# One inversion for both softmax sums and a new order of the first batch's twelve small products

## The chip, the cores and the metric

One core of a Trainium2 chip runs the whole kernel. The metric is the device time of one execution in microseconds (us); the profile of one execution gives the span from the first to the last instruction, some 2 us less. Engines are TensorE (PE in the profile), VectorE (DVE), ScalarE (ACT), GpSimd (POOL, which here issues all loads but two) and SyncE.

## The reference, cut to what matters

```python
def _attn_ref(q, k, v, tau):                 # B, N, C = 4, 6016, 256
    qn = q / (np.linalg.norm(q, axis=1, keepdims=True) + 1e-06)
    kn = k / (np.linalg.norm(k, axis=1, keepdims=True) + 1e-06)
    s = kn.transpose(0, 2, 1) @ qn / tau     # 256 x 256 per batch
    s = s - s.max(-1, keepdims=True)
    a = np.exp(s)
    a /= a.sum(-1, keepdims=True) + 1e-09
    return v @ a

def _moe_ref(x, w_gate, w_val, w_out):       # x: 24064 x 256, d_ff = 1536
    gate = 1.0 / (1.0 + np.exp(-(x @ w_gate)))
    val = x @ w_val
    return gate * val @ w_out
```

The kernel never forms `v @ a`. Per batch it multiplies the 256 x 256 matrix `a` into the weights, G = a·w_gate and H = a·w_val, and then runs the gated network on `v` itself.

Of the kernel before, what the change touches and what calls it, by code (L numbers as in the profile page):

```python
# [9 lines left out]
FP32 = mybir.dt.float32  # L10
# [7 lines left out]
def kernel(  # L18
# [20 lines left out]
    nc = tc.nc  # L39
    P = nc.NUM_PARTITIONS  # L40
# [8 lines left out]
    CB = C // P  # L49
    FC = DFF // P  # L50
    FG = 512
# [17 lines left out]
    def pool(name, bufs, **kw):  # L69
        return ctx.enter_context(tc.tile_pool(name=name, bufs=bufs, **kw))  # L70
# [4 lines left out]
    attp = pool("attp", 1)  # L75
# [6 lines left out]
    psg = pool("psg", 2, space=PSUM)  # L82
    psv = pool("psv", 2, space=PSUM)
    pso = pool("pso", 2, space=PSUM)
    pss = pool("pss", 1, space=PSUM)
    psm = pool("psm", 1, space=PSUM)
# [3 lines left out]
    def mm(out, lhsT, rhs, start, stop, **kw):  # L90
        nc.tensor.matmul(out, lhsT=lhsT, rhs=rhs, start=start, stop=stop, **kw)  # L91
# [23 lines left out]
    t0, nt = groups0[0]  # L115
# [15 lines left out]
    ones_bf = consts.tile([P, P], BF16)  # L131
# [26 lines left out]
    st = {}  # L158

    def invert(out, x, eps, num):  # L160
        nc.vector.tensor_scalar(out=out, in0=x, scalar1=eps, scalar2=None, op0=ALU.add)
        nc.vector.reciprocal(out, out)
# [175 lines left out]
        s.setdefault("e", []).append(e)  # L338
        s.setdefault("rrow", [])

    def sums(b, i, pl=psm, tag="m"):
        s = st[b]
        ps_r = pl.tile([P, 1], FP32, tag=tag, name="ps_r")
        for j in range(CB):
            mm(ps_r, s["e"][i][:, j, :], ones_bf[:, 0:1], j == 0, j == CB - 1)
        r = attp.tile([P, 1], FP32, tag=f"rrow{i}", name="rrow", bufs=2)
        invert(r, ps_r, 1e-9, 1.0)
        s["rrow"].append(r)

    def sums_both(b):  # L350
        s = st[b]
        ps_r = psm.tile([P, CB], FP32, tag="m", name="ps_r")
        for i in range(CB):
            for j in range(CB):
                mm(
                    ps_r[:, i : i + 1],
                    s["e"][i][:, j, :],
                    ones_bf[:, 0:1],
                    start=(i == 0 and j == 0),
                    stop=(j == CB - 1),  # L360
                    skip_group_check=True,
                )
        r = attp.tile([P, CB], FP32, tag="rrow", name="rrow", bufs=2)
        invert(r, ps_r, 1e-9, 1.0)
        s["rrow"] = [r[:, i : i + 1] for i in range(CB)]

    def gh_tiles(b):
        st[b]["gh"] = [
            [ghpool.tile([P, CB, FG], BF16, tag=f"{n}{fg}", name=f"gh_{n}{fg}") for fg in range(NFG)]
            for n in ("G", "H")  # L370
        ]

    gh_order = [(fg, w, i) for fg in range(NFG) for w in range(2) for i in range(CB)]

    def gh(b, n, pl=None, tag=None, act=None):
        s = st[b]
        fg, w, i = gh_order[n]
        ps = (pl or psm).tile([P, FG], FP32, tag=tag or "m", name="ps_gh")
        for j in range(CB):
            mm(  # L380
                ps,
                s["e"][i][:, j, :],
                w_sb[w][fg][:, j, :],
                start=(j == 0),
                stop=(j == CB - 1),
            )
        dst = s["gh"][w][fg][:, i, :]
        r = s["rrow"][i]
        if act if act is not None else n % 2 == 0:
            nc.scalar.activation(out=dst, in_=ps, func=ACT.Copy, scale=r)  # L390
        else:
            nc.vector.tensor_scalar(out=dst, in0=ps, scalar1=r, scalar2=None, op0=ALU.mult)  # L392


    vts = {}

    def transpose_v(b, ci, ps=None, late=None):

        t0, nt = chunks[ci]
        v_sb = vs.pop((b, ci))  # L400
        vT = vtpool.tile([P, TPC * CB, P], BF16, tag="vT", name="vT")
        flat = v_sb[:, :nt, :].rearrange("p t c -> p (t c)")
        if ps is None:
            nc.sync.dma_start_transpose(out=vT[:, : nt * CB, :], in_=flat)
        else:
            for n in range(nt * CB):
                nc.tensor.transpose(
                    out=ps[:, n, :], in_=flat[:, ds(n * P, P)], identity=ident_bf
                )
            half = nt * CB // 2  # L410
            (nc.scalar.copy if late is None else late)(vT[:, half : nt * CB, :], ps[:, half : nt * CB, :])
            nc.vector.tensor_copy(out=vT[:, :half, :], in_=ps[:, :half, :])
        vts[b, ci] = vT.rearrange("p (u cb) n -> p cb u n", cb=CB)

    hts = {}

    def glu(b, ci, f):
        t0, nt = chunks[ci]
        n = nt * P
        G, H = st[b]["gh"]  # L420
        vT = vts[b, ci]
        if f == 0:
            hts[b, ci] = hpool.tile([P, FC, CH], BF16, tag="hT", name="hT")
        ps_gate = psg.tile([P, CH], FP32, tag="g", name="ps_gate")
        ps_val = psv.tile([P, CH], FP32, tag="v", name="ps_val")
        for ps, w in ((ps_gate, G), (ps_val, H)):
            for ib in range(CB):
                mm(
                    ps[:, :n],
                    w[f // (FG // P)][:, ib, ds(f % (FG // P) * P, P)],  # L430
                    vT[:, ib, :nt, :],
                    start=(ib == 0),
                    stop=(ib == CB - 1),
                )
        g_sb = gpool.tile([P, CH], BF16, tag="g", name="g_sb")
        nc.scalar.activation(out=g_sb[:, :n], in_=ps_gate[:, :n], func=ACT.Sigmoid)  # L436
        nc.vector.tensor_tensor(  # L437
            out=hts[b, ci][:, f, :n], in0=ps_val[:, :n], in1=g_sb[:, :n], op=ALU.mult
        )
# [3 lines left out]
    def out_mms(b, ci, n0, n1):  # L443

        t0, nt = chunks[ci]
        hT = hts[b, ci]
        for n in range(n0, min(n1, nt * FC)):
            s, f = divmod(n, FC)
            if n == 0:
                ffn[b, ci] = opool.tile([P, TPC, C], FP32, tag="osb", name="out_sb")  # L450
            if f == 0:
                ffn["ps"] = pso.tile([P, C], FP32, tag="o", name="ps_o")
            mm(ffn["ps"], hT[:, f, ds(s * P, P)], w_out_sb[:, f, :], f == 0, f == FC - 1)
            if f == FC - 1:
                pending.append((ffn[b, ci], s, ffn["ps"], b, ci))
# [3 lines left out]
    def flush():  # L459
        while pending:  # L460
            out_sb, s, ps, b, ci = pending.pop(0)
            t0, nt = chunks[ci]
            nc.vector.tensor_copy(out=out_sb[:, s, :], in_=ps)  # L463
            if s == nt - 1:
                nc.sync.dma_start(out=out_rows[b][:, t0 : t0 + nt, :], in_=out_sb[:, :nt, :])
# [29 lines left out]
    for g, (t0, nt) in enumerate(groups0):  # L495
# [6 lines left out]
        while adds:  # L502
            w, last_sq = adds.pop()
# [28 lines left out]
    weights(0, 1)  # L532
    late = []
    transpose_v(
        0, 0, psv.tile([P, TPC * CB, P], BF16, tag="v", name="ps_tp"), lambda *a: late.append(a)
    )
    nc.scalar.copy(*late.pop())
    gh_tiles(0)
    sums(0, 0)
    gh(0, 0, psg, "g", act=False)  # L540
    sums(0, 1, pss, "s")
    gh(0, 1, psg, "g", act=True)
    gh(0, 2, psv, "v", act=False)
    gh(0, 3, psv, "v", act=True)
    nc.scalar.preload_act_table(ACT.Sigmoid)  # L545
    gh(0, 4, pso, "o", act=False)


    def side_work(b):
# [47 lines left out]
        return side  # L597


    prev = None  # L600
    for b in range(B):
        side = side_work(b)
        for ci in range(NCH):
            block = b + 1 < B and ci in (9, 10)
            for f in range(FC):
                glu(b, ci, f)
                flush()
                if prev is not None and not block:
                    out_mms(*prev, f * TPC, (f + 1) * TPC)
                for fn, a in side.get((ci, f), ()):  # L610
                    fn(*a)
                if (b, ci) == (0, 0) and f < len(gh_order) - 5:
                    gh(0, 5 + f, pso, "o")
            if prev is not None and block:
                for s in range(TPC):
                    for fn, a in side.get((ci, FC + s), ()):
                        fn(*a)
                    out_mms(*prev, s * FC, (s + 1) * FC)
                    flush()
            prev = (b, ci)  # L620
# [39 lines left out]
```

## The kernel before: what the change touches

The six pieces of G and H (three groups of 512 columns each) are cut into two row blocks, so there are twelve products, numbered 0 to 11 in the code and called first to twelfth here. Each is two matmuls of 512 columns into one bank of PSUM (a bank here is one buffer of a PSUM pool in the code: `psg`, `psv` and `pso` have two, `psm` and `pss` one), then one eviction that scales by the inverse softmax sum, on ScalarE or VectorE.

```python
gh_order = [(fg, w, i) for fg in range(NFG) for w in range(2) for i in range(CB)]   # 3 x 2 x 2

def gh(b, n, pl=None, tag=None, act=None):
    ...                                          # two matmuls into ps
    if act if act is not None else n % 2 == 0:
        nc.scalar.activation(out=dst, in_=ps, func=ACT.Copy, scale=r)
    else:
        nc.vector.tensor_scalar(out=dst, in0=ps, scalar1=r, scalar2=None, op0=ALU.mult)

def glu(b, ci, f):                               # one slot: 128 of the 1536 hidden columns
    ...
    ps_gate = psg.tile([P, CH], FP32, tag="g", name="ps_gate")     # 2 banks
    ps_val = psv.tile([P, CH], FP32, tag="v", name="ps_val")       # 2 banks
    for ps, w in ((ps_gate, G), (ps_val, H)):
        ...                                      # a pair of matmuls each
    nc.scalar.activation(out=g_sb[:, :n], in_=ps_gate[:, :n], func=ACT.Sigmoid)
    nc.vector.tensor_tensor(out=hts[b, ci][:, f, :n], in0=ps_val[:, :n], in1=g_sb[:, :n], op=ALU.mult)
...
gh_tiles(0)
sums(0, 0)                                       # sum and inversion of row block 0
gh(0, 0, psg, "g", act=False)
sums(0, 1, pss, "s")                             # sum and inversion of row block 1
gh(0, 1, psg, "g", act=True)
gh(0, 2, psv, "v", act=False)
gh(0, 3, psv, "v", act=True)
nc.scalar.preload_act_table(ACT.Sigmoid)
gh(0, 4, pso, "o", act=False)
...
for f in range(FC):                              # 12 slots to a chunk of v
    glu(b, ci, f)
    ...
    if (b, ci) == (0, 0) and f < len(gh_order) - 5:
        gh(0, 5 + f, pso, "o")                   # sixth to twelfth, slots 0 to 6; pso has 2 banks
```

The first chunk of `v` has three row tiles (matmuls of 384 columns), the others four (512). The second chunk is transposed on TensorE in slot 8 and copied from PSUM half by ScalarE and half by VectorE; later chunks are transposed by DMA. In later batches the twelve products run beside other work and the change does not touch them.

## Time and profile before

| | before |
|---|---|
| time, median of 6 runs | 830.18 us (829.89 to 830.55) |
| span of the profiled run | 827.9 us |
| first exponential starts | 35.03 us |
| first of the twelve products starts | 35.66 us |
| second chunk's first gate pair starts | 50.50 us |
| from there to the end | 777.40 us |

The table splits the run at three places: everything ahead of the first exponential is loading and the scores, which the change does not touch, the stretch of 15 us to the second chunk is where the change acts, and the rest would show whether a gain is given back. The lines behind it are in the prediction.

### The profile page before, as it was taken

Reading aid. Unit: us, or ns where it says so; the run is one execution under the profiler, and the core shown is the slowest. Engines: PE = TensorE matmul, PEld = TensorE weight load, DVE = VectorE, ACT = ScalarE, POOL = GpSimd, SP = SyncE. Lnnn points to the kernel's source line nnn. Section 1 sums busy time; section 2 is a strip of 40 time slices with the busy share of each in tenths; the row PEclk is TensorE's granted clock in tenths of the full one; section 3 lists DMA queues with packets and bytes.
Section 4 is the critical chain, followed back from the end, with each engine's and each line's share of the span. In section 5 each row is a group of like instructions: output and inputs, shape, how many; then the busy total and the mean of one; then the engine's idle time right before and its main releaser. Section 6 shows DMA issues by size and latency. Waiting matters only on the chain.

```text
span 827.9 us, 13618 instructions
## 1 busy us (share of the span) xinstructions
PE 806.3 (97%) x5120; PEld 498.2 (60%) x5132; DVE 589.7 (71%) x1025; ACT 392.0 (47%) x644; POOL 79.0 (10%) x151
## 2 busy tenths in 40 slices
PE   3899999999999999999999999999999999999998
PEld 2555666655666666665656566666656656666665
DVE  5777787777667777778757777778766666666664
ACT  3754444446544444445654444444565444444442
POOL 4532100002210100000301100000000000000000
PEclk9999999999999999999999999999999999999999
DMA  9999833229836532223965632232232423222111
GB/s 213 206 204 177 133 89 64 50 51 182 142 73 136 99 61 58 52 68 74 167 121 128 121 71 51 65 77 59 53 87 51 65 64 76 59 67 62 39 48 69
DMA packets 78130, 77.24 MB, mean 93 GB/s; under 512 B 50928, under 2 KB 56048, under 8 KB 78064
## 3 DMA queue, kind: packets, MB, share of 16 engines
q0 software_dynamic: 22768, 38.81, 28.4%
q1 hardware_dynamic: 55008, 36.97, 17.4%
q8 instruction: 40, 0.66, 0.3%
q10 hardware_dynamic: 288, 0.59, 0.2%
q14 instruction: 26, 0.21, 0.1%
HBM read 78.64 MB, written 24.64 MB: 125 GB/s over the span
## 4 chain that ended last, share of the span: by engine, by line
PE 93%; DMA 3%; DVE 1%; ACT 1%; issue 0%; POOL 0%; POOLq 0%; ACTq 0%
PE ps_o L91 30%; PE ps_val L91 29%; PE ps_gate L91 29%; PE ps_s L91 4%; DMA k_sb<-in_k_dram 3%; PE ps_gh L91 2%; DVE hT L437 1%; ACT g_sb L436 0%; DVE sq L187 0%; PE ps_n L91 0%; POOL q_sb L101 0%; PE ps_end L91 0%; ACT L545 0%; POOL k_sb L101 0%; DVE gh_G L392 0%
## 5 line engine op out<-in xcount | busy, mean ns | idle before, releaser
L437 DVE TENSOR_TENSOR hT<-ps_val,g_sb 128x512 bf16<-128x512 f32 (+1 forms) x576 | 390.7, 679 | 205.9 <-ACT g_sb L436 204.1
L436 ACT ACTIVATE g_sb<-ps_gate 128x512 bf16<-128x512 f32 (+1 forms) x576 | 338.2, 588 | 385.2 <-PE ps_gate L91 372.4
L91 PE MATMUL ps_val<-vT,gh_H 128*128 128x512 bf16 (+1 forms) x1152 | 337.7, 375 | 0.7 <-DVE gh_H L392 0.2
L91 PE MATMUL ps_gate<-vT,gh_G 128*128 128x512 bf16 (+1 forms) x1152 | 337.5, 375 | 0.2
L91 PE MATMUL ps_o<-w_out_sb,hT 128*128 128x256 bf16 x2244 | 324.3, 273 | 0.0
L91 PEld LDWEIGHTS <-hT 128*128 128x128 bf16 x2268 | 221.0, 98 | 125.3
L91 PEld LDWEIGHTS <-gh_H 128*128 128x128 bf16 x1152 | 112.7, 98 | 132.8 <-issue 1.8
L91 PEld LDWEIGHTS <-gh_G 128*128 128x128 bf16 x1152 | 112.5, 98 | 37.5 <-issue 0.2
L463 DVE COPY out_sb<-ps_o 128x256 f32<-128x256 f32 x187 | 77.3, 413 | 13.4 <-PE ps_o L91 13.4
L91 PE MATMUL ps_s<-k_sb,q_sb 128*128 128x256 bf16 x376 | 69.6, 287 | 16.4 <-DMA k_sb<-in_k_dram 9.3
L111 POOL DMA_DIRECT2D v_sb<-in_v_dram x48 | 25.6, 532 | 604.2 <-DMA vT<-v_sb 475.2
L91 PEld LDWEIGHTS <-q_sb 128*128 128x128 bf16 x376 | 38.5, 103 | 24.7 <-issue 10.3
L226 DVE TENSOR_TENSOR acc<-acc,sq 128x1024 bf16<-128x1024 bf16 (+1 forms) x66 | 44.2, 669 | 0.0
L187 DVE TENSOR_TENSOR sq<-q_sb 128x1024 bf16<-128x1024 bf16 (+2 forms) x42 | 28.0, 666 | 1.2 <-DMA q_sb<-in_q_dram 1.1
L101 POOL DMA_DIRECT2D q_sb<-in_q_dram x44 | 24.4, 555 | 29.6 <-PE ps_s L91 12.0
L101 POOL DMA_DIRECT2D k_sb<-in_k_dram x44 | 24.1, 547 | 18.0 <-DMA k_sb<-in_k_dram 9.4
L187 DVE TENSOR_TENSOR sq<-k_sb 128x1024 bf16<-128x1024 bf16 (+2 forms) x34 | 22.4, 658 | 0.2 <-DMA k_sb<-in_k_dram 0.2
L185 ACT ACTIVATE sq<-k_sb 128x1024 bf16<-128x1024 bf16 (+1 forms) x11 | 10.7, 1010 | 12.0 <-DMA k_sb<-in_k_dram 12.0
L91 PE MATMUL ps_gh<-w_val,e_sb 128*128 128x512 bf16 x45 | 13.5, 379 | 0.2
L91 PE MATMUL ps_gh<-w_gate,e_sb 128*128 128x512 bf16 x41 | 12.7, 379 | 0.4 <-DMA w_gate<-in_moe_w_gate_dram 0.2
L91 PEld LDWEIGHTS <-e_sb 128*128 128x128 bf16 x112 | 10.0, 97 | 4.5 <-ACT e_sb L327 1.0
L436 ACT ACT_TABLE_LOAD x6 | 7.7, 1283 | 9.4 <-PE ps_gate L91 9.3
(69 smaller groups left out, 122.9 us busy)
## 6 DMA issues: line engine op xcount, KB each, us to landing
out_dram<-out_sb SPq DMA_DIRECT2D x43, 512.0 KB, 2.9
v_sb<-in_v_dram POOLq DMA_DIRECT2D x44, 256.0 KB, 3.9
q_sb<-in_q_dram POOLq DMA_DIRECT2D x35, 256.0 KB, 6.6
k_sb<-in_k_dram POOLq DMA_DIRECT2D x35, 256.0 KB, 7.6
q_sb<-in_q_dram POOLq DMA_DIRECT2D x4, 512.0 KB, 11.6
k_sb<-in_k_dram POOLq DMA_DIRECT2D x4, 512.0 KB, 13.5
out_dram<-out_sb SPq DMA_DIRECT2D x5, 384.0 KB, 2.5
v_sb<-in_v_dram POOLq DMA_DIRECT2D x4, 192.0 KB, 3.5
```

The lines of the kernel that those rows point to most:

```text
L91: nc.tensor.matmul(out, lhsT=lhsT, rhs=rhs, start=start, stop=stop, **kw)
L101: nc.gpsimd.dma_start(out=tl[:, :nt, :], in_=rows(src, b)[:, t0 : t0 + nt, :])
L111: nc.gpsimd.dma_start(out=v_sb[:, :nt, :], in_=rows(v, b)[:, t0 : t0 + nt, :])
L185: nc.scalar.activation(out=sq[:, :nt, :], in_=src[:, :nt, :], func=ACT.Square)
L187: engine.tensor_tensor(out=sq[:, :nt, :], in0=src[:, :nt, :], in1=src[:, :nt, :], op=ALU.mult)
L226: nc.vector.tensor_tensor(out=acc[:, :nt, :], in0=acc[:, :nt, :], in1=st[b]["sq", w][:, :nt, :], op=ALU.add)
L436: nc.scalar.activation(out=g_sb[:, :n], in_=ps_gate[:, :n], func=ACT.Sigmoid)
L437: nc.vector.tensor_tensor(out=hts[b, ci][:, f, :n], in0=ps_val[:, :n], in1=g_sb[:, :n], op=ALU.mult)
L463: nc.vector.tensor_copy(out=out_sb[:, s, :], in_=ps)
```

## The change

It does four things, of which the title does not name the last. It inverts both sums together, after the first product's matmuls; it puts the fifth product between the gate and the value pair of slot 0; it puts the eleventh and the twelfth product into slot 5 together; and it gives the copy of the second chunk's transposed `v` whole to VectorE.

```diff
-    sums(0, 0)
-    gh(0, 0, psg, "g", act=False)
-    sums(0, 1, pss, "s")
+    ps_first = gh_mms(0, 0, psg, "g")
+    sums_both(0)
+    gh_store(0, 0, ps_first, False)
     gh(0, 1, psg, "g", act=True)
     ...
     nc.scalar.preload_act_table(ACT.Sigmoid)
-    gh(0, 4, pso, "o", act=False)
     ... (transpose_v)
-            half = nt * CB // 2
-            (nc.scalar.copy if late is None else late)(vT[:, half : nt * CB, :], ps[:, half : nt * CB, :])
+            half = nt * CB // 2 if late else nt * CB
+            if late:
+                late(vT[:, half : nt * CB, :], ps[:, half : nt * CB, :])
             nc.vector.tensor_copy(out=vT[:, :half, :], in_=ps[:, :half, :])
     ... (glu, in the loop over gate and value)
+            if between is not None and w is G:
+                between()
     ... (main loop)
+    gh_first = {f: (5 + f,) for f in range(len(gh_order) - 7)}
+    gh_first[len(gh_order) - 7] = tuple(range(len(gh_order) - 2, len(gh_order)))
-                glu(b, ci, f)
+                first = (b, ci, f) == (0, 0, 0)
+                glu(b, ci, f, (lambda: gh(0, 4, pso, "o", act=False)) if first else None)
-                if (b, ci) == (0, 0) and f < len(gh_order) - 5:
-                    gh(0, 5 + f, pso, "o")
+                if (b, ci) == (0, 0):
+                    for i in gh_first.get(f, ()):
+                        gh(0, i, pso, "o")
```

(Cuts are marked; `gh` is split into its matmuls and its eviction, and `sums` goes away.)

More of the change, by code (lines that the diff above doesn't have):

```diff
@@ L339, in exps @@
         s.setdefault("rrow", [])
-    def sums(b, i, pl=psm, tag="m"):
-        s = st[b]
-        ps_r = pl.tile([P, 1], FP32, tag=tag, name="ps_r")
-        for j in range(CB):
-            mm(ps_r, s["e"][i][:, j, :], ones_bf[:, 0:1], j == 0, j == CB - 1)
-        r = attp.tile([P, 1], FP32, tag=f"rrow{i}", name="rrow", bufs=2)
-        invert(r, ps_r, 1e-9, 1.0)
-        s["rrow"].append(r)
     def sums_both(b):
@@ L373, with gh_mms @@
     gh_order = [(fg, w, i) for fg in range(NFG) for w in range(2) for i in range(CB)]
-    def gh(b, n, pl=None, tag=None, act=None):
+    def gh_mms(b, n, pl, tag):
         s = st[b]
         fg, w, i = gh_order[n]
-        ps = (pl or psm).tile([P, FG], FP32, tag=tag or "m", name="ps_gh")
+        ps = pl.tile([P, FG], FP32, tag=tag, name="ps_gh")
         for j in range(CB):
@@ L386, in gh, with gh_store @@
             )
+        return ps
+    def gh_store(b, n, ps, act):
+        s = st[b]
+        fg, w, i = gh_order[n]
         dst = s["gh"][w][fg][:, i, :]
         r = s["rrow"][i]
-        if act if act is not None else n % 2 == 0:
+        if act:
             nc.scalar.activation(out=dst, in_=ps, func=ACT.Copy, scale=r)
@@ L392, in gh @@
             nc.vector.tensor_scalar(out=dst, in0=ps, scalar1=r, scalar2=None, op0=ALU.mult)
+    def gh(b, n, pl, tag, act=None):
+        gh_store(b, n, gh_mms(b, n, pl, tag), n % 2 == 0 if act is None else act)
     vts = {}
@@ L415, with glu @@
     hts = {}
-    def glu(b, ci, f):
+    def glu(b, ci, f, between=None):
         t0, nt = chunks[ci]
```

## The prediction

> **What bounds the kernel now.** I read the page first, then TensorE's list of waits, then the chain of work in the 20 us that the diff touches, then the timeline of TensorE, VectorE and ScalarE there.
>
> The page's first line, and what TensorE waited for in the whole run (line waited for, total us, times, longest):
>
> ```profile
> PE 806.3 (97%) x5120; PEld 498.2 (60%) x5132; DVE 589.7 (71%) x1025; ACT 392.0 (47%) x644; POOL 79.0 (10%) x151
> PE ps_s L91 <- DMA k_sb<-in_k_dram: 9.3, 6, 3.0
> PE ps_s L91 <- ACT k_sb L139: 7.0, 1, 7.0
> PE ps_r L91 <- ACT e_sb L327: 0.5, 1, 0.5
> PE ps_gh L91 <- DMA w_gate<-in_moe_w_gate_dram: 0.2, 1, 0.2
> PE ps_val L91 <- DVE gh_H L392: 0.2, 1, 0.2
> ```
>
> TensorE is busy for 806.3 of 827.9 us. Of its 21.6 us of idle time, 16.3 belong to loading the first batch, before anything that this change touches. From 50 us to the end the same list is empty. So the change, which alters only 35 to 51 us, can win at most the small holes of that stretch. The chain of work there (start, us, what):
>
> ```profile
> 35.80 0.47 PE ps_gh L91 x2
> 36.30 0.75 DVE gh_G L392
> 37.05 0.08 DVE rrow L161
> 37.15 0.18 DVE rrow L162
> 37.41 0.69 ACT gh_G L390
> 38.10 0.58 ACT gh_H L390
> 38.69 1.28 ACT L545
> 39.99 0.50 ACT g_sb L436
> 40.51 0.57 DVE hT L437
> 41.12 0.48 PE ps_val L91 x2
> ...
> 47.02 0.67 DVE gh_H L392
> 47.73 0.34 PE ps_val L91
> ```
>
> The reader is to see two excursions away from TensorE. In the first, the second inversion (37.05 to 37.33) stands behind the eviction of the first product on VectorE. ScalarE's first eviction waits for it until 37.41, and then come its second eviction, the sigmoid table's load and the first sigmoid. In the second, the value product of slot 8 waits for the twelfth product, evicted only at 47.0. The rest is in the timelines:
>
> ```profile
> 37.90 0.59 PE L91 MATMUL ps_gh<-w_gate,e_sb 128*128 128x512 bf16 x2 [0.23 <-DMA w_gate<-in_moe_w_gate_dram]
> 44.77 0.74 DVE L392 TENSOR_SCALAR gh_G<-ps_gh,rrow 128x512 bf16<-128x512 f32 x1
> 49.17 0.42 DVE L412 COPY vT<-ps_tp 128x512 bf16<-128x512 bf16 x1 [0.44 <-ACT vT L411]
> 49.65 0.49 PE L91 MATMUL ps_gate<-vT,gh_G 128*128 128x384 bf16 x2
> 50.18 0.48 PE L91 MATMUL ps_val<-vT,gh_H 128*128 128x384 bf16 x2
> ```
>
> **Holes, from starts rather than idle time.** A matmul's recorded end overlaps the next one, so I take spacing. Two 512-column matmuls follow at 0.43 us (36.18 to 36.61 and the like), two 384-column ones at 0.33 (48.35, 48.68, 49.00). Against that:
> - The fifth product starts at 37.90. The four before it, begun at 36.65, leave room from 37.52: 0.38 us lost, on a weight load.
> - Slot 2's value product starts at 41.12, its gate pair at 40.53: 0.59 less 0.33 is 0.26 lost, waiting for slot 0's product on VectorE to free its bank.
> - Slot 8's second value matmul starts at 47.73, its first at 47.22: 0.51 less 0.16 is 0.35 lost.
> - Slot 11's value pair starts at 50.18, its gate pair at 49.65: 0.53 less 0.33 is 0.20 lost, because VectorE is late after the v copy.
>
> Together 1.19 us: 0.14% of the kernel, the ceiling of the change.
>
> [...] the first gate pair, whose operand was ready at 38.10, starts at 38.33 behind the fifth product that was held to 37.90. [...] The load took 1.28 us, but it began 0.01 after the eviction before it and the sigmoid began 0.02 after it; [...] so I count 1.28. [...] VectorE's half of the v copy stood 0.44 us behind ScalarE's half of the same bank.
>
> **The change, part by part.**
>
> *One inversion.* Two tiny matmuls, one add and one reciprocal on VectorE go away as separate steps (0.15 + 0.16 us of work); the remaining pair takes 128x2 operands at 0.15 and 0.17, as later batches show. It now needs both exponentials. The second ends at 36.05; its sum matmuls started at 36.12 before and should again, ending at 36.32. Before, the sum's end (35.80) to the add's start took 0.04, and from the add's start to the scaled eviction 0.46 on VectorE (35.84 to 36.30) and 0.44 on ScalarE (36.97 to 37.41). So the add starts at 36.36, VectorE's first eviction at 36.82 instead of 36.30, ScalarE's first at 36.83 instead of 37.41. ScalarE's second is then held by its own product, whose matmuls end at 37.67 as before: it starts at 37.72 and ends at 38.40 instead of 38.68. Of 0.58 us won on the first, 0.28 reach the table load. First sigmoid: 39.71. First hT: 40.22 to 40.79. Slot 2's value product: 40.83 instead of 41.12, a gain of 0.29 that TensorE really sees.
>
> *Fifth product moved.* The gate pair now needs both G parts, ready at 37.57, and starts about 37.62 instead of 38.33. The fifth product follows at 37.95, just after its weights at 37.90. The value pair waits for H (38.40) and starts at 38.45 to 38.50 instead of 38.66. TensorE's early gain of about 0.2 lies in front of the 40.83 above, so it is inside the 0.29 and not added: it is what keeps the fifth product out of the way, not time by itself.
>
> *Last two products in one slot.* The twelfth leaves slot 6 for slot 5, about 0.9 us earlier, so slot 8 finds its H: plus 0.35. But these products have two banks. The tenth, in slot 4, is evicted by VectorE at 44.77 to 45.51, shifted by 0.29 to 44.48 to 45.22. The eleventh would start at 44.44 and the twelfth at 44.87, in the tenth's bank: it must wait to about 45.27, minus 0.40. This new wait is my main doubt.
>
> *The v copy of the second chunk*, which the short title does not name: ScalarE's half (0.58 us) goes, and VectorE copies all 1024 columns. The rows give 0.35 us for 384 columns and 0.42 for 512, so 0.57 ns a column and 0.71 us for 1024. VectorE does 0.29 more work but loses the wait of 0.44, and ScalarE is 0.58 freer for the next sigmoid. I expect slot 11's hole to close: plus 0.20.
>
> Sum: 0.29 + 0.35 + 0.20 - 0.40 = 0.44 us; without the bank wait 0.84. I take a gain of 0.55 us.
>
> **Rivals.**
> - *The bank wait takes back everything* (0.6 us or more, if the twelfth lands in the eleventh's bank or the tenth's eviction comes later than shifted). For it: only 0.43 lies between the two products against an eviction of 0.74. Against it: TensorE waiting there lets the sigmoids catch up, and slot 8's wait still goes. Time: 830.2 to 830.4.
> - *VectorE becomes the bound of the first chunk.* Per slot it has 0.56 for hT plus every other 0.74, under 1 us of the slots' 1.09 (43.00 to 44.08); the longer v copy is one step of 0.71. In slots 8 to 11, spaced 0.65, there is little room: hT of slot 9 might come late again. Then slot 11 keeps its 0.20 hole: gain 0.25, 830.05.
> - *A transfer hides the gain.* The DMA queues are full until 70 us. But q of batch 1 was issued at 37.18 with a median of 12.3 us to landing, so it is there by about 49.5, first used at 54.40. The third chunk's v transpose was issued at 48.23 and took 15.7, so it lands at 63.9 and is first needed at 66.10: 2.2 us of slack against a shift below 1.2. This would have to fail by more than 1 us; I give it little. Time then 830.3.
> - *Everything closes*: 1.19 us, 829.1. Against: the table load still stands in series after 38.40.
>
> **Range and chances.** 830.3 less 0.55 is 829.75. Mechanisms spread from 829.1 to 830.4. Three runs of the same kernel spread over 829.89 to 830.55, so 0.3 to 0.5 us of run-to-run noise goes on both sides: 828.9 to 830.7. A 2% change is 16.6 us, fourteen times all the holes that the change can reach: within 2% is 0.99, and the rest covers a mistake about the later batches, whose program I read as unchanged.
>
> **What would show it.** One inversion of 128x2 starting at about 36.36; ScalarE's first eviction at 36.83 and the table load at about 38.41; the first gate pair at 37.6 and the fifth product between it and its value pair; slot 2's value pair at about 40.83; a hole of about 0.4 before the twelfth product; none in slots 8 and 11; one v copy of 128x1024 at about 0.71 us on VectorE; the second chunk's first gate pair at about 50.0 instead of 50.50, and the same lead kept to the end. I am wrong if that lead is under 0.1 or over 1.0 us, if TensorE gets a wait after 51 us, or if the lead is there at 51 us and gone at the end.

No term of the sum goes with them: it came to 0.29 + 0.35 + 0.20 - 0.40 = 0.44 us, raised to 0.55, and the 1.28 us of the table load behind the 0.29 is the trace's own. "Full until 70 us" is there as a DMA share of 1.07 to 1.27 in each 10 us from 10 to 70 us.

## The result, and the profile after

| | before | after |
|---|---|---|
| time, median of 6 runs each | 830.18 us (829.89 to 830.55) | 829.73 us (829.33 to 830.03) |
| ratio, 95% interval | | 0.9994 (0.9981 to 1.0007) |
| span of the profiled run | 827.9 us | 828.3 us |
| first exponential starts | 35.03 us | 35.80 us |
| first exponential to second chunk's first gate pair | 15.47 us | 15.04 us |
| from there to the end | 777.40 us | 777.46 us |

The ratio is the mean time of one kernel's fast runs over that of the other's of the same rounds, so it is not quite the ratio of the two medians. Its interval contains 1: by the times alone, this change cannot be told from none. The medians differ by 0.45 us.

The two profiled spans have the wrong sign, and the reader should see why before trusting any span. These are the same 11 us of loading, before and after; behind the window come its length, the busy time of the five engines with instruction counts, the granted TensorE clock, the DMA share and GB/s:

```profile
20.00:31.00 11.00, 7.46 (x47) 5.41 (x48) 8.90 (x14) 7.32 (x8) 3.81 (x7) 0.84 1.10 208
```

```profile
20.00:31.00 11.00, 8.43 (x40) 5.72 (x41) 8.86 (x14) 7.44 (x8) 3.93 (x7) 0.55 1.10 207
```

In the run that was profiled after the change the granted clock was 0.55 instead of 0.84 there, fewer matmuls got done (40 against 47), and the first exponential came 0.77 us later. Nothing in that stretch was changed. The chain of work says that it was the matmuls: ahead of the first exponential it ends in a load of k before (20.78 to 31.77 us), and in that run it goes through the score matmuls from 25.35 to 33.21 us. So all times below count from the first exponential, or from the first product.

What TensorE waited for in the changed kernel, over the whole run (one more line, 0.2 us of "issue" during the scores, is left out):

```profile
PE 808.0 (98%) x5120; PEld 499.4 (60%) x5132; DVE 590.2 (71%) x1023; ACT 391.8 (47%) x643; POOL 78.9 (10%) x151
PE ps_s L91 <- DMA k_sb<-in_k_dram: 8.1, 4, 3.0
PE ps_s L91 <- ACT k_sb L139: 6.9, 1, 6.9
PE ps_gh L91 <- ACT e_sb L327: 0.5, 1, 0.5
PE ps_gh L91 <- DVE gh_G L388: 0.2, 1, 0.2
```

The waits for the fifth product's weights and for H in slot 8 are gone. A new one stands in the last line: a product that waits for the eviction of another. The chain of work in the stretch (L386 and L388 are now the evictions, L548 the sigmoid table, L438 and L439 the sigmoid and hT):

```profile
36.36 0.60 PE ps_gh L91 x2
36.96 0.11 PE ps_r L91 x4
37.08 1.33 PE ps_gh L91 x6
38.43 0.69 ACT gh_H L386
39.13 1.28 ACT L548
40.43 0.50 ACT g_sb L438
40.95 0.57 DVE hT L439
41.56 0.48 PE ps_val L91 x2
...
45.30 0.67 DVE gh_G L388
46.01 0.59 PE ps_gh L91 x2
```

The inversion is out of the chain: it goes from the sums straight through TensorE's products to ScalarE's second eviction. The table load still stands in series (1.31 us from the end of the eviction before it, at 39.12, to the sigmoid at 40.43; the load itself is 1.28), and slot 2's value pair starts 5.76 us after the first exponential (41.56 less 35.80) against 6.09 before. The second excursion has a new form: at the end of it is now the twelfth product at 46.01, 0.04 after the end of the tenth's eviction (45.30 + 0.67 = 45.97). In the timeline:

```profile
45.17 0.59 PE L91 MATMUL ps_gh<-w_val,e_sb 128*128 128x512 bf16 x2
46.01 0.59 PE L91 MATMUL ps_gh<-w_val,e_sb 128*128 128x512 bf16 x2 [0.24 <-DVE gh_G L388]
49.26 0.68 DVE L412 COPY vT<-ps_tp 128x1024 bf16<-128x1024 bf16 x1
50.16 0.49 PE L91 MATMUL ps_gate<-vT,gh_G 128*128 128x384 bf16 x2
50.52 0.48 PE L91 MATMUL ps_val<-vT,gh_H 128*128 128x384 bf16 x2
```

The eleventh and twelfth product start 0.84 us apart where 0.43 is their work: 0.41 lost. (The view prints an idle time of 0.24, since a recorded matmul end runs past the next one's start, here by 0.16, 0.59 recorded against a spacing of 0.43; spacing of starts is the measure.) The copy of `v` is one step of 0.68 on VectorE, and slot 11's pairs are 0.36 apart where 0.33 is work: its hole of 0.20 is down to 0.03.

The book of holes, in us: slot 2's value pair 0.33 earlier, slot 8's hole 0.35 gone, slot 11's reduced by 0.17, the new wait 0.41. Sum 0.33 + 0.35 + 0.17 - 0.41 = 0.44, against 15.47 - 15.04 = 0.43 measured over the stretch.

### The profile page after: what moved, and what is told of

Same layout as the page of the kernel before. It is cut to its first block, busy times and chain, and to the rows that moved or that the text cites. A ratio compares the mean times of both kernels' runs of the same rounds, so it can differ in the third digit from the quotient of the medians.

```text
span 828.3 us, 13614 instructions
## 1 busy us (share of the span) xinstructions
PE 808.0 (98%) x5120; PEld 499.4 (60%) x5132; DVE 590.2 (71%) x1023; ACT 391.8 (47%) x643; POOL 78.9 (10%) x151
## 4 chain that ended last, share of the span: by engine, by line
PE 94%; DMA 2%; DVE 1%; ACT 1%; POOL 1%; issue 0%; POOLq 0%
PE ps_o L91 30%; PE ps_val L91 29%; PE ps_gate L91 29%; PE ps_s L91 4%; DMA k_sb<-in_k_dram 2%; PE ps_gh L91 2%; DVE hT L439 1%; ACT g_sb L438 0%; POOL q_sb L101 0%; DVE sq L187 0%; PE ps_n L91 0%; POOL k_sb L101 0%; PE ps_end L91 0%; ACT L548 0%; PE ps_busy L91 0%
## 5 line engine op out<-in xcount | busy, mean ns | idle before, releaser
L439 DVE TENSOR_TENSOR hT<-ps_val,g_sb 128x512 bf16<-128x512 f32 (+1 forms) x576 | 391.3, 680 | 205.0 <-ACT g_sb L438 202.7
L438 ACT ACTIVATE g_sb<-ps_gate 128x512 bf16<-128x512 f32 (+1 forms) x576 | 338.2, 588 | 386.1 <-PE ps_gate L91 373.4
L91 PE MATMUL ps_s<-k_sb,q_sb 128*128 128x256 bf16 x376 | 71.9, 295 | 15.2 <-DMA k_sb<-in_k_dram 8.1
```

Of the source, the lines that this page charges most:

```text
L91: nc.tensor.matmul(out, lhsT=lhsT, rhs=rhs, start=start, stop=stop, **kw)
```

## The experiments

My theory was this sum: four local waits, each with its own cause, and nothing given back after 51 us. The rivals were that the gain is chance, that the new wait is VectorE being late rather than a bank, and that some part's gain belongs to another part. Nine runs were made, of eight kernels (the changed one twice more), all correct. Two yardsticks are used: E, from the first exponential's start, and W, from the first product's start, to the second chunk's first gate pair.

| run | E, us | W, us | rest to the end, us | holes left in the stretch, us |
|---|---|---|---|---|
| before | 15.47 | 14.84 | 777.40 | slot 2 0.26, slot 8 0.35, slot 11 0.20 |
| after | 15.04 | 14.48 | 777.46 | slot 2 0.26, twelfth product 0.41 |
| after_again | 15.66 | 14.44 | 777.37 | slot 2 0.26, twelfth product 0.41 |
| after_more | 15.08 | 14.52 | 777.38 | slot 2 0.26, twelfth product 0.41 |
| own_banks | 14.66 | 14.09 | 777.37 | slot 2 0.26 |
| fifth_first | 15.17 | 14.61 | 777.35 | slot 2 0.13, eighth product 0.15, twelfth 0.41 |
| inv_only | 15.80 | 14.54 | 777.41 | slot 2 0.26, slot 8 0.35, slot 11 0.20 |
| vcopy_only | 15.94 | 14.68 | 777.43 | slot 2 0.26, slot 8 0.35 |
| pair_only | 15.75 | 15.13 | 777.39 | eighth product 0.25, twelfth 0.40, slot 11 0.19 |
| fill_only | 15.00 | 14.44 | 777.43 | third product 0.31, slot 3 0.30 |
| tight | 14.96 | 13.73 | 777.46 | none over 0.10 |

A hole is the spacing of two starts less the work between them; holes ahead of the fifth product or first gate pair are left out, except the one of fill_only. Each row is one trace. W leaves out what the new order gains ahead of the first product: it starts 0.56 us after the first exponential, against 0.63 before, when two small sum matmuls stood ahead of it. So where no load holds the first product, W shows 0.07 less gain than E (0.36 against 0.43).

**after_again and after_more: the changed kernel again.** No edit.

> The changed kernel, unaltered, for more rounds. Yardstick: from the start of the first exponential to the start of the second chunk's first gate pair, 15.47 us before (35.03 to 50.50) and 15.04 changed (35.80 to 50.84). My theory (four local waits: -0.33, -0.35, -0.17, +0.41) expects 15.04 again within 0.05, and a time 0.3 to 0.6 us under the kernel before. Rival (the 0.45 us between the medians is chance, or is given back later): the stretch repeats but the times' ratio is 1.0000 or above.

> The changed kernel once more, for the times only. Yardstick now from the first product's start (not the exponential's, since in some traces the first weight block lands later than the exponential) to the second chunk's first gate pair: 14.84 us before, 14.48 and 14.44 in the two traces of the changed kernel. My theory: 14.44 to 14.50, and 777.3 to 777.5 us from there to the end as in all eight traces. Rival (the gain is given back late): the remainder is over 777.7.

after_again took 829.92 us (829.47 to 830.33, 5 runs) against 830.13 (9 runs), ratio 0.9998 (0.9985 to 1.001); after_more 829.56 (829.36 to 830.25, 5 runs) against 830.13 (9 runs), ratio 0.9995 (0.9982 to 1.0007). Two expectations failed in after_again: the time is 0.21 us under before and not 0.3 to 0.6, and E is 15.66, which is longer than before's 15.47. The trace says why:

```profile
PE ps_gh L91 <- DMA w_gate<-in_moe_w_gate_dram: 1.1, 1, 1.1
36.09 0.59 PE L91 MATMUL ps_gh<-w_gate,e_sb 128*128 128x512 bf16 x2 [1.12 <-DMA w_gate<-in_moe_w_gate_dram]
```

Here the first product waited for its weights, which landed at 36.09, while the first exponential was done at 35.38. This happened in four of the eleven traces (after_again, inv_only, vcopy_only, tight; first product at 36.09 to 36.15), with both orders of the code, and it does not happen in the trace of before that I predicted from. From the first product on, after_again is like the others: 14.44 against 14.48 and 14.52. So E was the wrong yardstick where the weights are late, and W, chosen after these traces had been seen, is used from here on. In after_more W is 14.52, just outside the 14.44 to 14.50 that I expected; the rest to the end is as expected. The mean over the three sets of runs of the changed kernel is 829.77 us (16 runs), and over all runs of the kernel before 830.13 (31 runs): 0.36 us, near the 0.43 of the traces, though no single comparison separates them. An estimate from these runs alone (standard deviations 0.33 and 0.23) is 0.36 with 0.19 on either side at 95%; it takes the runs as independent and leaves out differences between chips and rounds. The rest to the end is 777.35 to 777.46 in all eleven traces: nothing is given back.

**own_banks: is the new wait a bank and nothing else?** The twelfth product goes into the bank that held the sums, free by then.

```diff
-                        gh(0, i, pso, "o")
+                        gh(0, i, *((psm, "m") if i == len(gh_order) - 1 else (pso, "o")))
```

> The changed kernel with the twelfth product in the bank that the sums used, free by then, so that it need not wait for the eviction of the tenth. My theory (the hole of 0.41 us before the twelfth product is the wait for a bank and nothing else): the hole goes, the stretch is 14.63, the time 0.4 us under the changed kernel. Rival (VectorE is late there anyway, so the hole only moves to a value pair of slots 6 to 8, or to slot 11): stretch 14.9 to 15.04, a new hole of 0.15 us or more on the value pairs.

Measured: the hole is gone. TensorE runs both products in one piece:

```profile
44.55 1.03 PE L91 MATMUL ps_gh<-w_val,e_sb 128*128 128x512 bf16 x4
45.42 0.49 PE L91 MATMUL ps_gate<-vT,gh_G 128*128 128x384 bf16 x2
```

Four matmuls take the 0.87 us from 44.55 to 45.42 that four are worth, E is 14.66 (14.63 expected), W 14.09 against 14.48, and no other hole appears. The rival that VectorE is late anyway falls. Time 829.50 us (829.05 to 829.67, 5 runs), ratio to before 0.9992 (0.9979 to 1.0006); the changed kernel's median of the same rounds (after_again) is 829.92, so 0.42 more, as expected, but within the noise.

**fifth_first: the move of the fifth product undone.**

```diff
+    gh(0, 4, pso, "o", act=False)
     ...
-                glu(b, ci, f, (lambda: gh(0, 4, pso, "o", act=False)) if first else None)
+                glu(b, ci, f)
```

> The changed kernel with only the fifth product moved back, ahead of the first gate pair. My theory (the move gives no time by itself, because slot 2's value pair waits for the sigmoid table in both orders): slot 2's value pair stays 5.76 us after the first exponential's start, the stretch stays 15.04. Rival (the move is worth the 0.2 us or more by which the first gate pair starts earlier): slot 2's value pair at 5.95 or later, stretch 15.2 to 15.3.

Slot 2's value pair starts at 5.77 us after the first exponential, as I expected and as the rival did not. But E is 15.17, not 15.04: the move is worth 0.13 after all, one product later (0.09 against after_more, whose exponential came as early as here, at 35.14). Its trace:

```profile
37.90 0.59 PE L91 MATMUL ps_gh<-w_gate,e_sb 128*128 128x512 bf16 x2
40.69 0.69 ACT L386 ACTIVATE gh_H<-ps_gh,rrow 128x512 bf16<-128x512 f32 x1
41.43 0.59 PE L91 MATMUL ps_gh<-w_val,e_sb 128*128 128x512 bf16 x2
```

The fifth product starts at 37.90 again, as in before (37.90) and pair_only (37.89), whose traces name its weights as the wait; this trace names nothing, but shows a hole of 0.29. With it everything behind on TensorE is later, so the seventh product's eviction on ScalarE starts 5.51 us after the first exponential (40.69 less 35.18) against 5.39 (41.19 less 35.80) in the changed kernel. It ends at 41.38, and the eighth product starts at 41.43: a wait of 0.15 where the changed kernel has 0.04. (It is the seventh product's bank that the eighth takes: in the changed kernel the sixth product's eviction still runs, from 41.43 to 42.17, when the eighth starts at 41.93, right after the seventh's has ended at 41.88. The two banks are not used strictly in turn.) I had followed only the wait that ends last at slot 2, not the one behind it. The loss hangs on that load: inv_only below has the old order too, its fifth product starts at 38.08 with a hole of only 0.10, and its eighth product waits 0.04. So the move pays where the fifth product's weights come late against the exponential, and these are single traces. Time 829.73 us (829.47 to 829.89, 4 runs), ratio 0.9995 (0.9981 to 1.0009).

**inv_only: the one inversion alone, on the kernel before.** The edit is the first hunk of the change.

> The kernel before with only the one inversion and its order of the first product (store after the inversion). My theory: ScalarE's first eviction starts 1.77 us after the first exponential instead of 2.38, its second is held by its own matmuls at about 2.65, slot 2's value pair at 5.76 to 5.80 instead of 6.09; holes of slots 8 and 11 stay (0.35 and 0.20): stretch 15.14 to 15.18. Rival (the inversion gains nothing by itself, the weight load of the fifth product holds TensorE): slot 2's value pair at 6.0 or later, stretch 15.4 or more.

The weights were late here too (first product at 36.15). So by the numbers written down beforehand the run lies on the rival's side: slot 2's value pair 6.42 us after the first exponential, a stretch of 15.80. But neither had reckoned with a load that holds the first product, so this test has to be read with W, which was chosen afterwards:

```profile
36.15 0.59 PE L91 MATMUL ps_gh<-w_gate,e_sb 128*128 128x512 bf16 x2 [1.16 <-DMA w_gate<-in_moe_w_gate_dram]
41.31 0.49 PE L91 MATMUL ps_val<-vT,gh_H 128*128 128x384 bf16 x2
```

From the first product, slot 2's value pair starts at 5.16 us, against 5.46 in before (weights in time) and in vcopy_only (weights late), and 5.20 in the changed kernel: the inversion alone carries the whole first gain of 0.3. Slots 8 and 11 keep their holes, and W is 14.54, 0.30 under before. Read so, the rival falls: the fifth product starts at 38.08, and slot 2 does not wait for it. The times do not show it: 830.12 us (829.91 to 830.17, 4 runs) against 830.13, ratio 1.0 (0.9986 to 1.0013).

**vcopy_only: the whole copy on VectorE alone, on the kernel before.** The edit is the hunk in `transpose_v`.

> The kernel before with only the second chunk's v copy given whole to VectorE. My theory: one copy of 128x1024 of about 0.68 us, no wait of VectorE for ScalarE, slot 11's hole 0.03 instead of 0.20; slot 8's hole of 0.35 stays; stretch (first exponential to the second chunk's first gate pair) 15.28 to 15.32 against 15.47. Rival (slot 11's hole is a late effect of slot 8's wait, not of the copy): hole 0.15 to 0.20 stays, stretch 15.45.

One copy of 0.68 us and no wait of VectorE for ScalarE; slot 8's hole stays at 0.35 and slot 11's goes (both pairs 0.36 apart, from 50.08 to 50.44):

```profile
49.08 0.68 DVE L413 COPY vT<-ps_tp 128x1024 bf16<-128x1024 bf16 x1
50.08 0.49 PE L91 MATMUL ps_gate<-vT,gh_G 128*128 128x384 bf16 x2
50.44 0.32 PE L91 MATMUL ps_val<-vT,gh_H 128*128 128x384 bf16 x1
```

So slot 11's hole belongs to the split copy, not to slot 8. W is 14.68, that is 0.16 under before, and E is out (15.94) for the same late weights. Time 829.84 us (829.62 to 830.09, 4 runs) against 830.17, ratio 0.9996 (0.998 to 1.0013).

**pair_only: the last two products in one slot, on the kernel before.**

```diff
-                if (b, ci) == (0, 0) and f < len(gh_order) - 5:
-                    gh(0, 5 + f, pso, "o")
+                if (b, ci) == (0, 0) and f < len(gh_order) - 6:
+                    for i in (5 + f,) if f < len(gh_order) - 7 else (5 + f, 6 + f):
+                        gh(0, i, pso, "o")
```

> The kernel before with only the last two products put into one slot. My theory: slot 8's hole (0.35) goes, a wait of 0.40 before the twelfth product comes, slot 11's hole of 0.20 stays: stretch 15.50 to 15.54 against 15.47, so alone this part gains nothing or loses a trifle. Rivals: the twelfth product's wait only takes up slack and slot 8's gain stays (15.15 to 15.25); or slot 11's hole goes too because slot 8's wait caused it (15.32).

As expected slot 8's hole goes, a wait of 0.40 takes its place, and slot 11 keeps 0.19. The stretch is longer than I had said (15.75 against 15.50 to 15.54), for a reason outside this part: the exponential came early here (34.76) while the fifth product's weights landed at 37.89 as ever, and the eighth product then waited 0.25 for a bank where before shows 0.04. Take that 0.21 off and 15.54 remains. That this part alone gains nothing rests on this correction. Time 829.91 us (829.69 to 830.42, 4 runs) against 830.17, ratio 0.9999 (0.9984 to 1.0014).

**fill_only: slot 2's hole filled with the eighth product.** On own_banks.

```diff
-                glu(b, ci, f, (lambda: gh(0, 4, pso, "o", act=False)) if first else None)
+                early = {0: lambda: gh(0, 4, pso, "o", act=False), 2: lambda: gh(0, 7, psm, "m")}
+                glu(b, ci, f, early.get(f) if (b, ci) == (0, 0) else None)
```

(The eighth product is left out at its old place.)

> The kernel with the twelfth product in a bank of its own, and besides the eighth product moved between slot 2's gate and value pairs, in that same free bank. My theory (slot 2's hole of 0.26 is the wait for slot 0's hT behind the sigmoid table, and can be filled with TensorE work, but VectorE then is late with slot 1's hT because the sixth product's eviction stands before it): slot 2's hole goes, a new hole of about 0.25 before slot 3's value pair, stretch from the first product 14.05 to 14.10 as without the move. Rival (any filling of the hole pays): stretch 13.8.

The hole of slot 2 went and a hole of 0.30 came before slot 3's value pair, at 42.17, right behind slot 1's hT on VectorE (41.57 to 42.12), which stands behind the sixth product's eviction. That is the theory. W is 14.44 and not 14.05 to 14.10: the third product, which takes the first block of w_val, started 0.31 after it could (at 36.85, with 0.15 of idle time that the trace puts down to the load of w_val), where the other traces have 0.06 or less there except pair_only. Without that load 14.13 would remain. Time 829.21 us (829.1 to 829.75, 4 runs) against 830.13, ratio 0.9991 (0.9975 to 1.0006).

**tight: the same, and the sixth product's eviction ahead of slot 0's hT.** VectorE is idle there, for 0.92 us before slot 0's hT in fill_only.

```diff
+        if behind is not None:       # in glu, ahead of the sigmoid
+            behind()
     ...
-                glu(b, ci, f, early.get(f) if (b, ci) == (0, 0) else None)
+                glu(b, ci, f, early.get(f) if (b, ci) == (0, 0) else None,
+                    (lambda: gh(0, 5, pso, "o")) if (b, ci, f) == (0, 0, 0) else None)
```

> As the run before, and the sixth product's eviction put ahead of slot 0's hT on VectorE, which is idle there. My theory: both holes go, stretch from the first product 13.75 to 13.85, time 0.3 us under the kernel with only the own bank and about 1.1 under the kernel before. Rival (VectorE's or ScalarE's queue moves the wait to slots 3 to 5): a new hole of 0.2 or more there, stretch 14.0 or more.

W is 13.73, 0.36 under own_banks and 1.11 under before. Both holes are closed; VectorE evicts two products in its idle time, and hT follows 0.16 later, when the sigmoid is done:

```profile
38.99 1.51 DVE L388 TENSOR_SCALAR gh_G<-ps_gh,rrow 128x512 bf16<-128x512 f32 x2 [0.37 <-PE ps_gh L91]
40.66 1.02 DVE L441 TENSOR_TENSOR hT<-ps_val,g_sb 128x384 bf16<-128x384 f32 x2 [0.16 <-ACT g_sb L440]
```

Time 829.20 us (828.80 to 829.66, 5 runs) against 830.13 (9 runs), ratio 0.9989 (0.9976 to 1.0001). The interval just reaches 1, so that it is faster than the kernels before and after the change is shown by the traces, and only made likely by the times; from fill_only, with 829.21 us, the times do not tell it at all. What lies ahead of the first product (loads, and a clock granted at 0.55 to 0.84 from 20 to 31 us) moves by nearly as much as all of this from run to run: that product starts at 35.38 to 36.36 us in the eleven traces.

## Why the prediction was right, point by point

- **Same within 2%, 829.75 us, range 828.9 to 830.7.** Measured 829.73. That it fits to 0.02 us is luck, with runs spreading over 0.7 us: the start was taken as 830.3, from three runs, where six have 830.18, and the gain as 0.55, where the medians have 0.45. That the sum of the parts fits is not luck.
- **Inversion, 0.29 us at slot 2.** The trace gives 0.33 (6.09 to 5.76 after the first exponential; 5.79 in after_more), of which 0.07 lies ahead of the first product, where I had none; inv_only, read from the first product, gives 0.30. The steps hold as well: relative to the exponential, ScalarE's first eviction was put at 1.80 and came at 1.77, its second at 2.69 and came at 2.63, the table load at 3.38 and came at 3.33. Two slips in the working changed nothing: 36.61 is the start of no matmul in the trace (the third product starts at 36.65; the spacing of 0.43 is there at 37.90 to 38.33), and the 0.44 from the add gives 36.80 for ScalarE's first eviction, not 36.83, which is the 1.77 that came.
- **Fifth product, "not time by itself".** This step failed, by 0.09 to 0.13. Slot 2 is indifferent to it as argued, but the eighth product's wait for a bank is not, where the fifth product's weights come late (fifth_first). Also the first value pair came earlier than argued (39.09 - 35.80 = 3.29 against 3.42 to 3.47): only its second matmul needs the second half of H, whose eviction ended at 39.12.
- **Last two in one slot, plus 0.35 and minus 0.40.** Measured plus 0.35 and minus 0.41; own_banks shows that the 0.41 is the bank.
- **The v copy, plus 0.20 at a cost of 0.71 on VectorE.** Measured 0.17 and 0.68.
- **The sum of 0.44, raised to 0.55.** The measured stretch is 0.43 shorter. The raise, a compromise with the case without a bank wait, had no ground: the bank wait came in full. In absolute time the sign that I gave did not come: the second chunk's first gate pair was put at about 50.0 us and started at 50.84, because the first exponential came 0.77 later.
- **Rivals.** The bank wait did not take back everything. VectorE did not become the bound. No later transfer hid the gain. What I did not see is a transfer ahead of the stretch: the first weight block lies near the bound itself, and in four of eleven traces it was the bound. From there on it changed nothing (W 14.44 in after_again against 14.48 and 14.52; slot 2's pair at 5.46 with it and without), so it blurred the comparison without turning it.

## What to carry to other kernels

When an engine is busy 97% of the time, list its holes by the spacing of starts, price each by what ends it, and the sum is an estimate of what any reordering can win; here 1.19 us, and a kernel that closes nearly all of them gained 1.11 in the trace. Here two products put into one slot needed a third bank, or the second waited 0.41 us for an eviction; before bundling work, count the banks against the eviction's length (0.74 us on VectorE here, with 0.43 between the two products). And measure a gain below the spread of the runs inside the trace, between two events of which the first lies behind everything that varies by itself.
